# Attention, experts and an MLP on one core: k and v loaded six tokens per partition, with new times in the attention's step list

## The chip, the cores and the metric

The kernel runs on one core of a Trainium2 chip. TensorE (PE, with its weight loads shown as PEld), VectorE (DVE), ScalarE (ACT), GpSimd (POOL) and SyncE (SP) run their own instruction lists in order and wait for one another at semaphores; DMA queues move data between DRAM and the cores' memory of 128 partitions. The metric is the device time of one execution in microseconds (us).

## The reference

Three stages follow one another: a linear attention over 4 batches of 8 heads with 576 tokens of 64 channels, a mixture of 8 experts that gives each of the 2,304 tokens to one expert, and an MLP with a softplus.

```python
kv  = einsum('bhsd,bhse->bhde', k, v)            # 64 x 64 for each head
out = einsum('bhsd,bhde->bhse', q, kv)
x   = out / sqrt(mean(out*out, -1) + 1e-6) * g_norm      # -> [2304, 512]

xn = x / (norm(x) + 1e-6)
logits = xn @ (emb / (norm(emb) + 1e-6)).T / tau          # 8 experts
e = argmax(logits); gate = softmax(logits)[e]
y = gate * (relu(x @ w1[e]) @ w2[e])                      # 512 -> 1024 -> 512

h = y @ w_in                                              # 512 -> 2048
out = (max(h, 0) + log1p(exp(-abs(h)))) @ w_out
```

All arrays are float32. The sum over tokens in kv takes the 576 tokens in any order and grouping.

## The kernel before

**Loads.** All loads of attention go through SP's queue in the order of the code: `load_kv(0, 4)`, q of batch 0 in two halves, k and v of batch 1 in two halves of four heads each, q of batch 1, and so on. A k or v tile is [128, 8 heads, 4*64]: 512 tokens, four on a partition, which is a piece of 1,024 bytes in DRAM. The rest of 64 tokens comes in tiles of its own, kr and vr, [64, 8, 64], in pieces of 256 bytes. Two buffers each serve four batches.

**Steps.** `kv_mm` sums a head's kv in PSUM: four matmuls with 128 rows (L295) and one with 64 (L296). `kv_fin` brings kv of a batch into kvx in six small steps ("fin") on ACT, DVE and PE. A tile t is 128 tokens; there are 18, of which tiles 8 and 13 are "mixed", made of the last 64 tokens of two batches. Each tile goes through q (a copy on DVE, L337), tr (transposes on PE), qs (a copy on ACT), o (matmuls with kvx, L354, or L358 for a mixed tile), sq (squares, ACT), cp (copy to oc, ACT), ss (sums, DVE, L371). Pairs of tiles then get a Newton step for the inverse root (n, DVE), lt and lg (logits, DVE), xa (the normalised tile, on POOL, written to the DRAM tensor xd as well), xo (times g_norm, **on POOL or DVE**, L410) and nn (squares of xo, ACT). `route(g)`, after each six tiles, finds the expert of each token (top-1, slots, tokens, on DVE and PE); behind the last one, ranks and indices make rk_e, the experts sorted by size, and rk_idx, the table of token rows of each expert (L541).

**The order.** Each step is entered with its engine, a time that it is supposed to cost, what it depends on, and for some an earliest time `at`, taken from the table `LATE`. `list_schedule` plays these numbers through and gives each step a begin and, for xo, an engine; the steps are then emitted in order of begin. On the chip nothing of these numbers remains but the order on each engine and the choice for xo. An xo that would end on POOL behind a threshold (53,000 in the table's ns) is put off by 10,000 there, so that DVE gets it.

**Behind attention.** POOL gathers the token rows of the first expert from xd by rk_idx, in three indirect DMAs into xgt (`gather`, L1038). SP loads weight pieces st once rk_e is known. PE transposes the gathered rows (`first_transposes`, L1068), ACT and DVE split them into xh and xl (L1072, L1076), weights are split into wh and wl (L857, L859), and from there PE multiplies experts and then the MLP to the end. Attention's tiles come from the pools hp and tp, which are closed at its end; xgt and st come from later pools that take the same memory over, opened with `reuse_waits="tile"`: the first writer of such a tile waits for the last instructions that used the old tiles lying there. Where a tile lies follows from the sizes allocated before it.

Of the kernel before, what the change touches and what calls it, by code (L numbers as in the profile page):

```python
# [11 lines left out]
F32 = mybir.dt.float32  # L12
# [13 lines left out]
def attention_moe_mlp(tc, q, k, v, g_norm, emb, tau, w1, w2, w_in, w_out, out, caps=CAPS):  # L26
# [7 lines left out]
    nc = tc.nc  # L34
# [145 lines left out]
    with ExitStack() as hs:  # L180
# [1 line left out]
        tp = hs.enter_context(tc.tile_pool(name="tp", bufs=1))  # L182
        ps = hs.enter_context(tc.tile_pool(name="ps", bufs=1, space=PSUM))

        kt, vt, qt, kr, vr, qr = {}, {}, {}, {}, {}, {}

        def load_kv(b, cuts=1):
            for dst, rem, nm in ((kt, kr, "k"), (vt, vr, "v")):
                dst[b] = hp.tile([128, H, 4 * D], F32, name=f"{nm}{b}", tag=f"{nm}{b % 2}")
                rem[b] = hp.tile([64, H, D], F32, name=f"{nm}r{b}", tag=f"{nm}r{b % 2}")  # L190
            for u in range(cuts):
                hs_ = slice(u * H // cuts, (u + 1) * H // cuts)
                for dst, rem, src in ((kt, kr, k), (vt, vr, v)):
                    nc.sync.dma_start(out=dst[b][:, hs_, :], in_=src[b, hs_, 0:512, :].rearrange("h (p c) d -> p h (c d)", c=4))
                    if u == 0:
                        nc.sync.dma_start(out=rem[b], in_=src[b, :, 512:576, :].rearrange("h p d -> p h d"))

        def load_q(b, half=None):
            if b not in qt:
# [85 lines left out]
        def kv_mm(b, heads, whole=True):  # L285

            for h in heads:
                key = (b, 0 if whole else h // 4)
                j = h // 2 if whole else h % 4 // 2
                if key not in kvs:  # L290
                    kvs[key] = misc_t[:, 0:4 * D].rearrange("p (j d) -> p j d", d=D) if whole else o_t[h // 4][:, 0:2, 0:D]
                kvo = kvs[key][64 * (h % 2):64 * (h % 2) + 64, j, :]
                for c in range(4):
                    cs_ = slice(c * D, c * D + D)
                    nc.tensor.matmul(kvo, kt[b][:, h, cs_], vt[b][:, h, cs_], start=c == 0, stop=False)  # L295
                nc.tensor.matmul(kvo, kr[b][:, h, :], vr[b][:, h, :], start=False, stop=True)  # L296

        kvts = tp.tile([128, 4, 128], F32, name="kvts")

# [48 lines left out]
        def st_o(t):  # L348

            lo, c = tiles[t]  # L350
            o, qs = o_t[t % 2], qs_t[t % NQS]
            for j in range(4):
                if c is not None:
                    nc.tensor.matmul(o[:, j, 0:144], qs[:, j, :], kvx[lo][:, j, :], start=True, stop=True)  # L354
                else:
                    for u in range(2):
                        us = slice(64 * u, 64 * u + 64)
                        nc.tensor.matmul(o[us, j, 0:144], qs[:, j, us], kvx[lo + u][:, j, :], start=True, stop=True)  # L358
# [218 lines left out]
        def step(key, engs, ns, fn, *deps, at=0, tail=0):  # L577

            steps_[key] = [engs, ns if isinstance(ns, tuple) else (ns,), fn, [d for d in deps if d in steps_], at, tail]

        LATE = {"kv1a": 2700, "kv1b": 5700, "q10": 7150, "q11": 8600, "kv2a": 13000, "kv2b": 15900, "qr0": 17400, "q20": 18850, "q21": 20300,
                "kv3a": 24600, "kv3b": 27600, "qr2": 29000, "q30": 30550, "q31": 32000}
        for b in range(1, B):
            step(("mm", b, 0), "P", 1670, lambda b=b: kv_mm(b, range(0, 4)), ("fin", b - 1, 5), at=LATE[f"kv{b}a"])
            step(("mm", b, 1), "P", 1670, lambda b=b: kv_mm(b, range(4, 8)), ("mm", b, 0), at=LATE[f"kv{b}b"])
            gen_ = kv_fin(b)
            mm = ("mm", b, 1)
            for i, (eng, ns, deps) in enumerate((
                ("A", 264, [mm]), ("D", 331, [mm]), ("P", 435, [("fin", b, 0), ("fin", b, 1)]),
                ("A", 478, [("fin", b, 2)]), ("P", 830, [("fin", b, 3)]), ("D", 131, [("fin", b, 4)]),  # L590
            )):
                step(("fin", b, i), eng, ns, lambda g_=gen_: next(g_), *deps)
# [31 lines left out]
        for t in range(NT):  # L624
            lo, c = tiles[t]
            p = t // 2
            if t > 1:
                if c is not None:
                    step(("q", t), "D", 335, lambda t=t: st_q(t), ("tr", t - NQC), at=LATE.get(f"q{lo}{c // 2}", 0))
                step(("tr", t), "P", 435, lambda t=t: st_tr(t), ("q", t), ("qs", t - 2), at=LATE[f"qr{lo}"] if c is None else 0)  # L630
                step(("qs", t), "A", 478, lambda t=t: st_qs(t), ("tr", t), ("o", t - NQS))
            step(("o", t), "P", 980 if c is not None else 1950, lambda t=t: st_o(t), ("qs", t), ("fin", lo if c is not None else lo + 1, 5), ("cp", t - 2), ("sq", t - 2), ("o", t - 1))
            step(("sq", t), "A", 478, lambda t=t: st_sq(t), ("o", t), ("ss", t - NSQ))
            step(("cp", t), "A", 531, lambda t=t: st_cp(t), ("o", t), ("lt", p - NOC), ("xa", 2 * (p - NOC)), ("xa", 2 * (p - NOC) + 1))
            step(("ss", t), "D", 610, lambda t=t: st_ss(t), ("sq", t), ("n", p - NSS, 2))
            if t % 2:
                step(("rs", p), "A", 460, lambda p=p: st_rs(p), ("ss", t - 1), ("ss", t), ("n", p - NSS, 2))
                gen_ = st_newton(p)
                for i in range(3):
                    step(("n", p, i), "D", 85, lambda g_=gen_: next(g_), ("rs", p) if i == 0 else ("n", p, i - 1), ("xa", 2 * (p - NSS)), ("xa", 2 * (p - NSS) + 1))  # L640
                step(("lt", p), "D", 202, lambda p=p: st_lt(p), ("n", p, 2), ("cp", t - 1), ("cp", t), ("lg", p - 2))
                step(("lg", p), "D", 202, lambda p=p: st_lg(p), ("lt", p))
                for u in (t - 1, t):
                    step(("xa", u), "G", 1001, lambda u=u: st_xa(u), ("n", p, 2), ("cp", u), ("xa", u - 1), tail=12000 if u == NT - 1 else 0)
                for u in (t - 1, t):
                    step(("xo", u), "GD", (1225, 560), lambda eng, u=u: st_xo(u, eng), ("xa", u), ("nn", u - NXO))
                    step(("nn", u), "A", 613, lambda u=u: st_n(u), ("xo", u))
            if t in ends:
                route(ends[t])

        def list_schedule():

            after = {k: [] for k in steps_}
            for k, v in steps_.items():
                for d in v[3]:
                    after[d].append(k)
            path = {}

            def length(k):
                if k not in path:  # L660
                    path[k] = steps_[k][1][0] + 180 + max(max((length(n) for n in after[k]), default=0), steps_[k][5])
                return path[k]

            free, begin, end, where = dict.fromkeys("PADG", 0), {}, {}, {}
            todo = dict.fromkeys(steps_)
            while todo:
                ready = []
                for k in todo:
                    engs, ns, _, deps, at, _ = steps_[k]
                    if all(d in end for d in deps):  # L670
                        best = None
                        for eng, n in zip(engs, ns):
                            lag = [end[d] + (220 if where[d] != eng else 0 if eng == "P" else 130) for d in deps]
                            t0 = max([free[eng], at] + lag)
                            if k[0] == "xo" and eng == "G" and t0 + n > 53000:

                                t0 += 10000
                            if best is None or t0 + n < best[3]:
                                best = (t0, k, eng, t0 + n)
                        ready.append(best)  # L680
                t0, k0, eng, t1 = min(ready, key=lambda r: (r[0], -length(r[1])))
                t0, k0, eng, t1 = max((r for r in ready if r[2] == eng and r[0] <= t0 + SLACK), key=lambda r: (length(r[1]), -r[0]))
                if k0[0] in ("nn", "xo"):

                    soon_ = [r for r in ready if r[2] == eng and r[0] < t0 + HOLD * (t1 - t0) and r[1][0] not in ("nn", "xo")]
                    if soon_:
                        t0, k0, eng, t1 = min(soon_, key=lambda r: r[0])
                begin[k0], end[k0], where[k0] = t0, t1, eng
                free[eng] = t1
                del todo[k0]  # L690
            return begin, where
# [696 lines left out]
```

## Time and profile before

| | |
|---|---|
| median of 3 runs | 761.85 us (760.89 to 762.2) |
| profiled execution | 759.51 us |
| its span, first to last instruction | 757.7 us |
| PE busy | 721.7 us (95%) |
| DVE, ACT, POOL busy | 531.3, 419.2, 269.4 us |
| DMA | 96.70 MB, 128 GB/s on average |
| attention, up to the index table | the first 92.6 us |

Busy shares over the whole span hide the stages: attention and the passage to the first expert make up the first 105 us, experts and MLP the rest. Times in the rows below are counted from the start of the span. A row `36.45 0.68 PE L295 ... x8` is a group of eight instructions of one line that starts at 36.45 and lasts 0.68 us; on PE the modelled ends overlap the next start, so what one costs is read from start to start. A float32 matmul of the program appears as two in the trace (x8 for four).

### The profile page before, as it was taken

The page shows a single profiled execution, that of the slowest core. Times are in us where ns is not written, and L with a number is a line of the kernel's source. Part 1 is how long each engine was busy: PE and PEld are TensorE (multiplying, and loading weights), DVE is VectorE, ACT ScalarE, POOL GpSimd, SP SyncE. Part 2 cuts the span into 40 slices and gives each one's busy share as a digit, 9 for nine tenths or more (in the row PEclk, how much of TensorE's full clock was granted, in tenths as well). Part 3 has the DMA queues.
Part 4 walks back from the last instruction along what each step waited for, and adds up shares of the span by engine and source line. Part 5 has one row for each costly group of instructions (what it writes and reads, how often), then busy time and mean ns, then how long its engine had stood idle before and what let it go on. Part 6 is the DMA issues. An engine that isn't in the chain of part 4 may idle for free.

```text
span 757.7 us, 11972 instructions
## 1 busy us (share of the span) xinstructions
PE 721.7 (95%) x4370; PEld 658.3 (87%) x4370; DVE 531.3 (70%) x1019; ACT 419.2 (55%) x821; POOL 269.4 (36%) x199
## 2 busy tenths in 40 slices
PE   9999269999999999998999999999999999999996
PEld 5888149989999999998999999999999989898985
DVE  4568977788787887897897565756665666575653
ACT  2657556646566576564765544644554464455443
POOL 3245645776776877673660100100010010001001
PEclk9999589999999999999999999999999999999998
DMA  9994298798988989941220100100010000001001
GB/s 237 266 257 173 85 342 272 248 294 265 297 276 283 303 272 314 292 135 43 98 84 1 42 1 0 43 1 1 0 43 1 1 28 15 1 0 43 1 1 45
DMA packets 71073, 96.70 MB, mean 128 GB/s; under 512 B 13010, under 2 KB 45802, under 8 KB 71008
## 3 DMA queue, kind: packets, MB, share of 16 engines
q1 hardware_dynamic: 67488, 86.02, 36.7%
q0 software_dynamic: 3344, 9.80, 3.6%
q8 instruction: 36, 0.59, 0.3%
q14 instruction: 29, 0.24, 0.1%
q10 hardware_dynamic: 176, 0.05, 0.0%
HBM read 78.01 MB, written 17.84 MB: 126 GB/s over the span
## 4 chain that ended last, share of the span: by engine, by line
PE 45%; issue 8%; DVE 1%; POOL 1%; ACT 0%; DVEq 0%; POOLq 0%
PE tp_t L853 8%; PE tp_t L852 8%; PE tp_t L851 8%; PE acc_t L957 7%; PE acc_t L956 7%; PE acc_t L955 7%; POOL out_dram L962 1%; DVE xsl L867 0%; DVE own L1265 0%; PE acc_t L853 0%; PE acc_t L851 0%; PE acc_t L852 0%; DVE eu L926 0%; ACT eu L923 0%; DVE x L1222 0%
## 5 line engine op out<-in xcount | busy, mean ns | idle before, releaser
L859 POOL TENSOR_TENSOR wl<-st,wh 128x1024 fp32r<-128x1024 f32 x66 | 159.0, 2410 | 74.7 <-ACT wh L857 73.9
L962 POOL DMA_INDIRECT out_dram<-orow,idx x18 | 19.9, 1103 | 337.2 <-ACT orow L961 333.8
L922 ACT ACTIVATE e<-tp_t 128x384 f32<-128x384 f32 x93 | 45.7, 492 | 127.8 <-PE tp_t L853 127.8
L924 DVE TENSOR_SCALAR u<-e 128x384 f32<-128x384 f32 x94 | 33.8, 360 | 112.5 <-ACT e L923 111.7
L857 ACT CAST wh<-st 128x1024 fp32r<-128x1024 f32 x72 | 75.2, 1048 | 44.8 <-POOL wl L859 17.4
L851 PE MATMUL acc_t<-hh,wh 128*128 128x368 f32 (+7 forms) x256 | 81.2, 317 | 1.2 <-DVE hl L1207 1.2
L851 PE MATMUL acc_t<-xh,wh 128*128 128x368 f32 (+7 forms) x256 | 78.6, 307 | 0.3 <-ACT x L1224 0.3
L852 PE MATMUL acc_t<-xl,wh 128*128 128x368 f32 (+7 forms) x256 | 78.2, 306 | 0.0
L853 PE MATMUL acc_t<-xh,wl 128*128 128x368 f32 (+7 forms) x256 | 78.0, 305 | 0.0
L853 PE MATMUL acc_t<-hh,wl 128*128 128x368 f32 (+7 forms) x256 | 78.0, 305 | 0.0
L852 PE MATMUL acc_t<-hl,wh 128*128 128x368 f32 (+7 forms) x256 | 78.0, 305 | 0.0
L930 ACT ACTIVATE u<-u 128x384 f32<-128x384 f32 x94 | 49.5, 526 | 50.0 <-DVE e L926 49.3
L852 PE MATMUL tp_t<-xsl,wh 128*128 128x384 f32 x192 | 64.6, 336 | 0.7 <-DVE xsl L867 0.7
L853 PE MATMUL tp_t<-xsh,wl 128*128 128x384 f32 x192 | 64.8, 337 | 0.0
L851 PE MATMUL tp_t<-xsh,wh 128*128 128x384 f32 x192 | 64.7, 337 | 0.0
L940 DVE TENSOR_TENSOR gl<-u,gh 128x384 fp32r<-128x384 f32 x94 | 60.2, 640 | 6.0 <-ACT gh L938 6.0
L853 PE MATMUL tp_t<-xsh,wl_b 128*128 128x384 f32 x188 | 63.4, 337 | 0.0
L851 PE MATMUL tp_t<-xsh,wh_b 128*128 128x384 f32 x188 | 63.3, 337 | 0.0
L852 PE MATMUL tp_t<-xsl,wh_b 128*128 128x384 f32 x188 | 63.2, 336 | 0.0
L957 PE MATMUL acc_t<-wh,gl 128*128 128x512 f32 x144 | 57.1, 397 | 1.6 <-DVE gl L940 1.6
L931 DVE SCALAR_TENSOR_TENSOR u<-tp_t,u 128x384 f32<-128x384 f32 x93 | 51.7, 556 | 9.9
L933 DVE TENSOR_TENSOR u<-u,e 128x384 f32<-128x384 f32 x94 | 56.0, 595 | 3.2
(254 smaller groups left out, 1880.3 us busy)
## 6 DMA issues: line engine op xcount, KB each, us to landing
st<-in_moe_w_dram SPq DMA_DIRECT2D x64, 512.0 KB
raw<-in_moe_w_in_dram SPq DMA_DIRECT2D x16, 512.0 KB
raw<-in_moe_w_out_dram SPq DMA_DIRECT2D x16, 512.0 KB
wd<-pre_p SPq DMA_DIRECT2D x32, 256.0 KB
q<-in_q_dram SPq DMA_DIRECT2D x8, 512.0 KB
xd<-xa SPq DMA_DIRECT2D x16, 256.0 KB
st<-wd SPq DMA_DIRECT2D x8, 512.0 KB
raw<-wd SPq DMA_DIRECT2D x8, 512.0 KB
```

Of the source, the lines that this page charges most:

```text
L851: nc.tensor.matmul(ps_, wh, xh, start=start, stop=False)
L852: nc.tensor.matmul(ps_, wh, xl, start=False, stop=False)
L853: nc.tensor.matmul(ps_, wl, xh, start=False, stop=stop)
L857: nc.scalar.copy(h, raw)
L859: eng.tensor_tensor(out=l, in0=raw, in1=h.bitcast(F32), op=ALU.subtract)
L930: nc.scalar.activation(out=u, in_=u, func=AF.Ln)
L931: nc.vector.scalar_tensor_tensor(out=u, in0=h, scalar=0.0, in1=u, op0=ALU.max, op1=ALU.add)
L933: nc.vector.tensor_tensor(out=u, in0=u, in1=e, op=ALU.subtract)
L940: nc.vector.tensor_tensor(out=gl, in0=u, in1=gh.bitcast(F32), op=ALU.subtract)
L955: nc.tensor.matmul(mt[b][t_], gh[:, cs_], wh[:, f % 2, :], start=f == 0, stop=False)
L956: nc.tensor.matmul(mt[b][t_], gh[:, cs_], wl[:, f % 2, :], start=False, stop=False)
L957: nc.tensor.matmul(mt[b][t_], gl[:, cs_], wh[:, f % 2, :], start=False, stop=f == NF - 1)
```

## The change

k and v tiles become [96, 8, 6*64]: six tokens on each of 96 partitions, a piece of 1,536 bytes, and all 576 tokens. The tiles of the rest and their eight DMAs go. A head's kv is six matmuls with 96 rows. The k and v tiles (two buffers each) take 12,288 bytes of a partition each instead of 8,192 and 2,048 for the rest. In the step list, the two kv steps of a batch are entered at 3,700 instead of 1,670, o at 1,180 (mixed: 1,500) instead of 980 (1,950), the threshold for xo on POOL is 60,000, and `LATE` has other times for kv, q and qr.

```diff
+        CK = 6
+        SK = S // CK
         def load_kv(b, cuts=1):
-            for dst, rem, nm in ((kt, kr, "k"), (vt, vr, "v")):
-                dst[b] = hp.tile([128, H, 4 * D], F32, name=f"{nm}{b}", tag=f"{nm}{b % 2}")
-                rem[b] = hp.tile([64, H, D], F32, name=f"{nm}r{b}", tag=f"{nm}r{b % 2}")
+            for dst, nm in ((kt, "k"), (vt, "v")):
+                dst[b] = hp.tile([SK, H, CK * D], F32, name=f"{nm}{b}", tag=f"{nm}{b % 2}")
             for u in range(cuts):
                 hs_ = slice(u * H // cuts, (u + 1) * H // cuts)
-                for dst, rem, src in ((kt, kr, k), (vt, vr, v)):
-                    nc.sync.dma_start(out=dst[b][:, hs_, :], in_=src[b, hs_, 0:512, :].rearrange("h (p c) d -> p h (c d)", c=4))
-                    if u == 0:
-                        nc.sync.dma_start(out=rem[b], in_=src[b, :, 512:576, :].rearrange("h p d -> p h d"))
+                for dst, src in ((kt, k), (vt, v)):
+                    nc.sync.dma_start(out=dst[b][:, hs_, :], in_=src[b, hs_].rearrange("h (p c) d -> p h (c d)", c=CK))
...
-                for c in range(4):
+                for c in range(CK):
                     cs_ = slice(c * D, c * D + D)
-                    nc.tensor.matmul(kvo, kt[b][:, h, cs_], vt[b][:, h, cs_], start=c == 0, stop=False)
-                nc.tensor.matmul(kvo, kr[b][:, h, :], vr[b][:, h, :], start=False, stop=True)
+                    nc.tensor.matmul(kvo, kt[b][:, h, cs_], vt[b][:, h, cs_], start=c == 0, stop=c == CK - 1)
...
-        LATE = {"kv1a": 2700, "kv1b": 5700, "q10": 7150, "q11": 8600, "kv2a": 13000, "kv2b": 15900, "qr0": 17400, "q20": 18850, "q21": 20300,
+        LATE = {"kv1a": 1700, "kv1b": 5800, "q10": 8000, "q11": 10200, "kv2a": 14300, "kv2b": 18400, "qr0": 19800, "q20": 22000, "q21": 24200,
...
-            step(("mm", b, 0), "P", 1670, lambda b=b: kv_mm(b, range(0, 4)), ("fin", b - 1, 5), at=LATE[f"kv{b}a"])
+            step(("mm", b, 0), "P", 3700, lambda b=b: kv_mm(b, range(0, 4)), ("fin", b - 1, 5), at=LATE[f"kv{b}a"])
...
-                            if k[0] == "xo" and eng == "G" and t0 + n > 53000:
+                            if k[0] == "xo" and eng == "G" and t0 + n > 60000:
```

How the lists change is seen at three places. The first is PE, before: the end of route 0's slot matmuls (oh_all is the chosen expert of each token), behind which the first kv matmuls of batch 3 stand (k3, v3). The mixed tile 8 stands before both, 21 rows up.

```order
L450 MATMUL rt_234<-oh_all_114,ones_68 128x16
L450 LDWEIGHTS ones_68
L450 MATMUL rt_234<-oh_all_114,ones_68 128x8
L295 MATMUL misc_233<-v3_211,k3_209 64x64 x4
L296 MATMUL misc_233<-vr3_212,kr3_210 64x64
```

The same place on PE, after: both kv steps of batch 3 (24 matmuls each), and then the mixed tile 8 (L357).

```order
L353 MATMUL o0_213<-kvx1_225,qs2_246 128x144 x4
L342 MATMUL qp1_216<-ident_70,qc3_243 128x128 x4
L295 MATMUL misc_217<-v3_198,k3_197 64x64 x24
L353 MATMUL o1_214<-kvx1_225,qs3_247 128x144 x4
L342 MATMUL qp0_215<-ident_70,qr0_191 128x128 x4
L295 MATMUL misc_217<-v3_198,k3_197 64x64 x24
L357 MATMUL o0_213<-kvx0_223,qs0_244 64x144
```

The kv matmuls of batch 3 have moved ahead of tile 8 and of route 0's slots. The second place is DVE at the end of attention, before: the index table and the xo products of the last two tiles, then the first row of what follows.

```order
L533 TENSOR_TENSOR pt_1079<-tab_311,perm_315 128x192
L541 TENSOR_REDUCE rk_idx_107<-pt_1079 128x24
L410 TENSOR_TENSOR xo6_291<-xa16_276,g_rep_227 128x512
L410 TENSOR_TENSOR xo7_292<-xa17_277,g_rep_227 128x512
L700 TENSOR_TENSOR below_1087<-rank_314,io8_79 128x64
```

DVE there, after:

```order
L532 TENSOR_TENSOR pt_1088<-tab_295,perm_299 128x192
L540 TENSOR_REDUCE rk_idx_107<-pt_1088 128x24
L409 TENSOR_TENSOR xo2_271<-xa12_256,g_rep_211 128x512
L409 TENSOR_TENSOR xo3_272<-xa13_257,g_rep_211 128x512
L409 TENSOR_TENSOR xo4_273<-xa14_258,g_rep_211 128x512
L409 TENSOR_TENSOR xo5_274<-xa15_259,g_rep_211 128x512
L409 TENSOR_TENSOR xo6_275<-xa16_260,g_rep_211 128x512
L409 TENSOR_TENSOR xo7_276<-xa17_261,g_rep_211 128x512
L699 TENSOR_TENSOR below_1103<-rank_298,io8_79 128x64
```

Six xo products stand behind rk_idx where two stood. The third place is POOL at the end of attention, before: the last xa, three xo, the three gathers and the first split of weights.

```order
L397 TENSOR_TENSOR xa17_277<-oc2_266,rinv2_306 128x512
L410 TENSOR_TENSOR xo3_288<-xa13_273,g_rep_227 128x512
L410 TENSOR_TENSOR xo4_289<-xa14_274,g_rep_227 128x512
L410 TENSOR_TENSOR xo5_290<-xa15_275,g_rep_227 128x512
L1038 DMA xgt_1128<-xd_60,rk_idx_107 128x512 x2
L1038 DMA xgt_1128<-xd_60,rk_idx_107 112x512
L859 TENSOR_TENSOR wl_0_1181<-st0_1132,wh_0_1179 128x1024
```

POOL there, after:

```order
L409 TENSOR_TENSOR xo1_270<-xa11_255,g_rep_211 128x512
L396 TENSOR_TENSOR xa14_258<-oc1_249,rinv1_289 128x512
L396 TENSOR_TENSOR xa15_259<-oc1_249,rinv1_289 128x512
L396 TENSOR_TENSOR xa16_260<-oc2_250,rinv2_290 128x512
L396 TENSOR_TENSOR xa17_261<-oc2_250,rinv2_290 128x512
L1037 DMA xgt_1144<-xd_60,rk_idx_107 128x512 x2
L1037 DMA xgt_1144<-xd_60,rk_idx_107 112x512
L858 TENSOR_TENSOR wl_0_1197<-st0_1148,wh_0_1195 128x1024
```

The three xo products between the last xa and the gathers are gone from POOL. In all, POOL has 11 of the 18 xo products before and 4 after; DVE has 7 and 14.

## Rows read from the trace of the kernel before

**Rows 1.** Busy time by stage: stretch, its length, engines, PE's granted clock, DMA share, GB/s

```profile
core 0: us, PE busy (x) PEld busy (x) DVE busy (x) ACT busy (x) POOL busy (x), PEclk, DMA share, GB/s
45.00:60.00 15.00, 14.13 (x151) 12.45 (x150) 13.76 (x36) 9.04 (x22) 8.94 (x7) 1.00 1.08 268
60.00:76.00 16.00, 14.05 (x135) 12.90 (x133) 14.38 (x40) 13.14 (x31) 9.59 (x9) 1.00 0.41 143
76.00:92.70 16.70, 3.17 (x37) 1.92 (x38) 15.67 (x44) 8.50 (x24) 10.42 (x9) 0.56 0.23 79
92.70:105.20 12.50, 7.63 (x27) 4.07 (x25) 7.31 (x24) 4.59 (x12) 5.58 (x4) 0.64 0.91 285
105.20:380.00 274.80, 268.89 (x1803) 258.72 (x1803) 222.35 (x363) 170.56 (x293) 190.11 (x95) 1.00 0.75 245
```

**Rows 2.** Waits of PE from 0 to 110 us: total, times, longest

```profile
PE acc_t L1068 <- DMA xgt<-xd,rk_idx: 4.9, 1, 4.9
...
PE o L296 <- DMA vr<-in_v_dram: 0.3, 1, 0.3
```

**Rows 3.** Timeline of PE at the kv matmuls of batch 2

```profile
36.45 0.68 PE L295 MATMUL misc<-v,k 128*64 128x64 f32 x8
37.06 0.33 PE L296 MATMUL misc<-vr,kr 64*64 64x64 f32 x2
37.31 0.68 PE L295 MATMUL misc<-v,k 128*64 128x64 f32 x8
```

**Rows 4.** Timeline of PE from attention's last o to the first expert

```profile
73.06 2.44 PE L354 MATMUL o<-kvx,qs 128*128 128x144 f32 x16
...
100.86 1.09 PE L1068 MATMUL acc_t<-ident,xgt 128*128 128x128 f32 x4 [4.87 <-DMA xgt<-xd,rk_idx]
101.74 1.06 PE L177 MATMUL tp_t<-ones 128*128 128x512 bf16 x2
...
104.30 0.58 PE L1068 MATMUL acc_t<-ident,xgt 112*128 112x112 f32 x2
104.68 0.58 PE L1068 MATMUL tp_t<-ident,xgt 112*128 112x112 f32 x2
...
113.91 0.74 PE L760 MATMUL tp_t<-tgb,sel_all 128*128 128x72 bf16 x18 [2.04 <-DVE tgb L756]
```

**Rows 5.** Timeline of DVE from 60 us to behind rk_idx

```profile
60.95 0.42 DVE L308 COPY kvx<-misc 64x256 f32<-64x256 f32 x1 [1.85 <-ACT kvx L306]
...
61.63 0.42 DVE L337 COPY qc<-q 128x512 f32<-128x512 f32 x1
...
63.07 0.95 DVE L337 COPY qc<-q 128x512 f32<-128x512 f32 x1
...
79.53 0.68 DVE L371 TENSOR_REDUCE ss<-sqb 128x8 f32<-128x520 f32 x1
...
87.93 1.08 DVE L460 TENSOR_SCALAR pm<-ci 128x6 int32<-128x6 int32 x1
88.92 0.16 DVE L461 TENSOR_SCALAR pm<-ci 128x6 int32<-128x6 int32 x1
...
89.07 0.94 DVE L464 TENSOR_TENSOR sel_all<-iota_i,pm 128x768 bf16<-128x768 int32 x1
...
92.26 0.35 DVE L541 TENSOR_REDUCE rk_idx<-pt 128x24 int32<-128x192 f32 x1
92.53 1.28 DVE L410 TENSOR_TENSOR xo<-xa,g_rep 128x512 f32<-128x512 f32 x2
93.73 0.21 DVE L700 TENSOR_TENSOR below<-rank,io 128x64 f32<-128x64 f32 x1
```

**Rows 6.** Timeline of POOL at the end of attention

```profile
85.28 3.70 POOL L410 TENSOR_TENSOR xo<-xa,g_rep 128x512 f32<-128x512 f32 x3
92.91 1.34 POOL L1038 DMA_INDIRECT xgt<-xd,rk_idx  x1 [3.94 <-DVE rk_idx L541]
```

**Rows 7.** SP's issues from 92 us, and GB/s from 92 to 106 us in 40 slices

```profile
92.57 2.22 SPq L1023 DMA_DIRECT2D st<-in_moe_w_dram  x4
...
GB/s 0 0 0 0 23 114 255 377 360 383 386 392 348 328 205 167 202 178 222 383 363 389 345 328 404 378 281 211 208 281 290 246 351 375 380 380 380 375 380 410
```

More of the change, by code (lines that the diff above doesn't have):

```diff
@@ L183, in attention_moe_mlp @@
         ps = hs.enter_context(tc.tile_pool(name="ps", bufs=1, space=PSUM))
-        kt, vt, qt, kr, vr, qr = {}, {}, {}, {}, {}, {}
+        kt, vt, qt, qr = {}, {}, {}, {}
+        CK = 6
+        SK = S // CK
         def load_kv(b, cuts=1):
-            for dst, rem, nm in ((kt, kr, "k"), (vt, vr, "v")):
-                dst[b] = hp.tile([128, H, 4 * D], F32, name=f"{nm}{b}", tag=f"{nm}{b % 2}")
-                rem[b] = hp.tile([64, H, D], F32, name=f"{nm}r{b}", tag=f"{nm}r{b % 2}")
+            for dst, nm in ((kt, "k"), (vt, "v")):
+                dst[b] = hp.tile([SK, H, CK * D], F32, name=f"{nm}{b}", tag=f"{nm}{b % 2}")
             for u in range(cuts):
                 hs_ = slice(u * H // cuts, (u + 1) * H // cuts)
-                for dst, rem, src in ((kt, kr, k), (vt, vr, v)):
-                    nc.sync.dma_start(out=dst[b][:, hs_, :], in_=src[b, hs_, 0:512, :].rearrange("h (p c) d -> p h (c d)", c=4))
-                    if u == 0:
-                        nc.sync.dma_start(out=rem[b], in_=src[b, :, 512:576, :].rearrange("h p d -> p h d"))
+                for dst, src in ((kt, k), (vt, v)):
+                    nc.sync.dma_start(out=dst[b][:, hs_, :], in_=src[b, hs_].rearrange("h (p c) d -> p h (c d)", c=CK))
         def load_q(b, half=None):
@@ L579, in step @@
             steps_[key] = [engs, ns if isinstance(ns, tuple) else (ns,), fn, [d for d in deps if d in steps_], at, tail]
-        LATE = {"kv1a": 2700, "kv1b": 5700, "q10": 7150, "q11": 8600, "kv2a": 13000, "kv2b": 15900, "qr0": 17400, "q20": 18850, "q21": 20300,
-                "kv3a": 24600, "kv3b": 27600, "qr2": 29000, "q30": 30550, "q31": 32000}
+        LATE = {"kv1a": 1700, "kv1b": 5800, "q10": 8000, "q11": 10200, "kv2a": 14300, "kv2b": 18400, "qr0": 19800, "q20": 22000, "q21": 24200,
+                "kv3a": 28300, "kv3b": 32400, "qr2": 33800, "q30": 36000, "q31": 38200}
         for b in range(1, B):
-            step(("mm", b, 0), "P", 1670, lambda b=b: kv_mm(b, range(0, 4)), ("fin", b - 1, 5), at=LATE[f"kv{b}a"])
-            step(("mm", b, 1), "P", 1670, lambda b=b: kv_mm(b, range(4, 8)), ("mm", b, 0), at=LATE[f"kv{b}b"])
+            step(("mm", b, 0), "P", 3700, lambda b=b: kv_mm(b, range(0, 4)), ("fin", b - 1, 5), at=LATE[f"kv{b}a"])
+            step(("mm", b, 1), "P", 3700, lambda b=b: kv_mm(b, range(4, 8)), ("mm", b, 0), at=LATE[f"kv{b}b"])
             gen_ = kv_fin(b)
@@ L631, in attention_moe_mlp @@
                 step(("qs", t), "A", 478, lambda t=t: st_qs(t), ("tr", t), ("o", t - NQS))
-            step(("o", t), "P", 980 if c is not None else 1950, lambda t=t: st_o(t), ("qs", t), ("fin", lo if c is not None else lo + 1, 5), ("cp", t - 2), ("sq", t - 2), ("o", t - 1))
+            step(("o", t), "P", 1180 if c is not None else 1500, lambda t=t: st_o(t), ("qs", t), ("fin", lo if c is not None else lo + 1, 5), ("cp", t - 2), ("sq", t - 2), ("o", t - 1))
             step(("sq", t), "A", 478, lambda t=t: st_sq(t), ("o", t), ("ss", t - NSQ))
```

## The prediction

> **What bounds the kernel now.** I read the windows by stage first [rows 1]. From 45 to 60 us the matrix engine (PE) is busy 14.13 of 15 us and VectorE (DVE) 13.76, so both are full. From 60 to 76 DVE is the fuller (14.38 of 16), and from 76 to 92.7 PE does almost nothing (3.17 of 16.7) while DVE is busy 15.67. From 92.7 to 105.2 neither is busy: this is the gather for the first expert. Behind 105.2 PE is busy again (268.89 of 274.8 us to 380), in code that the change leaves alone. So three things bound in turn: PE to about 60, DVE to the end of the index table rk_idx, then a gather through DRAM, then PE. What the change does to attention counts only as far as it moves rk_idx or the gather.
>
> PE's list of waits [rows 2] says what PE lacks. The largest single one, 4.9 us, is for the gathered rows xgt. For loads of k and v it waits once, 0.3 us at the start; all later ones are ahead of PE.
>
> The rows of DVE [rows 5] and POOL [rows 6] show the hand-over: rk_idx is written from 92.26 to 92.61, POOL issues the gather at 92.91 (0.30 later), and the first transpose of gathered rows runs at 100.86 [rows 4], 7.95 us after the issue.
>
> **The change, part by part.**
>
> *Matmuls of kv.* Before, four 128-row matmuls start 0.61 us ahead of the 64-row one, 0.152 each, and the 64-row one takes 0.25 to the next head's start [rows 3]: 0.86 a head. After, six matmuls of 96 rows. No row has 96; the nearest are the transposes [rows 4], where four of 112 rows and 112 columns take 0.38 per pair (0.19 each) and those of 128 take 0.22 each, so the time goes with the columns and fewer rows cost nothing extra. I take 0.152: 0.91 a head, +0.05 over 32 heads, **+1.4 us on PE**. Below: 0.114 (rows in proportion), −5.7 us. Above: 0.25 as the 64-row ones, +20 us. The +1.4 lies on PE before 60 us, where PE is full, but PE's last o matmuls end at 75.5 [rows 4], and DVE, which is behind with its rows, comes to the last ss that needs them at 79.53 [rows 5]. Less than about 4 us on PE thus stays hidden behind DVE's queue, and I put it at 0; without that cover it costs 1.4.
>
> *Loads.* Eight small DMAs of 64 tokens go, and k and v (9.4 MB of the 14.2 MB that are loaded) come in pieces of 1,536 bytes instead of 1,024 and 256. As PE waits for no load now [rows 2], a faster one gives nothing. A slower one is a rival.
>
> *The order on DVE from 60 us to rk_idx.* The new times and costs push PE's two kv steps of batch 3 ahead of the mixed tile 8 and of route 0's slot matmuls (the order rows of PE). DVE's answers move with them, and this is the part that a table of times hides. Counting DVE rows between that point and rk_idx, after against before: two more ss reductions (0.68 long as at 79.53; they and the xo products follow one another at 0.60): +1.2; route 0's slot chain, which before was done by 57.9, now falls in the stretch: one sel row at 0.94 and eight short ones at about 0.2 (as pm at 88.92): +2.5, an estimate; one more xo product: +0.6 (two take 1.20, from 92.53 to 93.73); one q copy (0.42) and one kvx copy (0.42) that are done before it: −0.8, of which I count −0.7 by their pitch [rows 5]. Sum **+3.6** of work.
>
> Against it stand two things. DVE idles 1.85 us for kvx just before 60.95; of that 0.95 lies after 60, and with DVE's work queued up it is filled: **−1.0**. And DVE is stretched by POOL: a q copy takes 0.95 at 63.07 and 0.42 at 61.63; pm takes 1.08 at 87.93, while POOL's three xo products run (85.28 to 88.98), and 0.16 at 88.92 when POOL is idle [rows 5, 6]. Between the first and the last of these two rows I count 11 such stretched DVE rows, their excess over the shortest row of their kind summing to 8.8 us. POOL works 9.59 + 10.42 = 20.0 us in the stretch [rows 1]; after, four xo products fewer run on it there (the order rows of POOL), some 1.3 us each: 5.2 us or 26% less, so **−2.3** of the 8.8. Bounds: half of the stretch goes (−4.4), or none of it. Sum for rk_idx: 3.6 − 1.0 − 2.3 = **+0.3 us** (−1.8 to +2.6).
>
> *The gather.* Here is the largest term, and the diff doesn't show it. The four k and v tiles grow from 10,240 bytes a partition (with their rests) to 12,288, so all that is allocated behind them moves up by 8 KB. The gather's buffer xgt lies in memory that attention's pool gives back: before on xa0 to xa3, whose last readers were long done; after on xa14 to xa17, whose last readers are their xo products. Those are now on DVE, six in a row right behind rk_idx, where two stood before (the order rows of DVE); four of them left POOL, where three xo products stood at the tail. In the built programs the first gather waits, before, for DVE's rk_idx; after, for the sixth xo. What is queued behind it on POOL is the other two gathers and wl of the first weights; PE waits for them. The price: the six start 0.08 before rk_idx's end as modelled [rows 5], five steps of 0.60 and a last one of 0.68 make 3.68, so the gather starts **+3.6 us** behind where it stood. Lower bound by the rows: none, as the six can't run in less than their pitch; upper: +4.6 if one of them is stretched by 1 us.
>
> *The landing.* The gather's rows then share the DMA queues with the weight loads that SyncE issues from 92.57 on: eight of 512 KB, moved at 330 to 410 GB/s from 93.4 on [rows 7], about 12 us. A gather issued 3.6 us later meets less of them. If it met none, its 0.75 MB would take some 2 us less; it still meets the last ones, so I take **−0.4** (0 to −2).
>
> *Behind the gather* the chains shift with it: transposes, xh and xl, then the gate table, whose PE wait of 2.04 us at 113.91 [rows 4] ends on DVE rows that are queued behind xl. Four more xo products ahead on DVE (+2.4) end before the gathered rows come.
>
> Sum: 0.3 + 3.6 − 0.4 = **+3.5 us**; the profiled execution took 759.51 us (a span of 757.7 and 1.8 around it), so 763.0. That execution lies 2.34 below the median of the runs, 761.85; on the median's scale the sum gives **765.3 us**. Ends: −1.8 + 3.6 − 2.0 = −0.2 and +2.6 + 4.6 = +7.2, or 761.6 to 769.1.
>
> **Rivals.**
>
> *Faster: DVE's tail shrinks by more than the gather waits.* The place is DVE between 60 and rk_idx. From 83.9 on its rows are one serial chain (top-1, slots, ranks, index), and three stretched ones stand in it; after, POOL has no xo products there. To be faster by more than 0.2% of the time (1.5 us, about what a measurement of this kernel can tell from no change; I use this bound throughout), rk_idx must come at 92.6 − 3.2 − 1.5 = 87.9 or earlier: more than half of the 8.8 us must go and the added 3.6 us of work must find idle time. With all stretches gone, the idle gone and 1 us of the work hidden: 3.6 − 1 − 1 − 8.8 = −7.2, net −4.0, about **758**. Against it: POOL still makes ten or so xa products, and these stretch DVE too. Chance 0.15.
>
> *No change: the later gather is absorbed.* PE's wait of 2.04 us at 113.91 is not for gathered rows but for the gate table on DVE. If that table comes no later than now, the wait shrinks by what PE comes later: 3.5 − 2.0 = +1.5, **763.3**; together with a landing that meets few weight loads, no change. For it: the table's inputs are ready at rk_idx and nn. Against: DVE takes its rows in order behind xl, and behind six xo products. Chance 0.18.
>
> *Slower loads.* With 96 of 128 partitions written, each k and v transfer could run at three quarters. From 45 to 60 us loads move 268 GB/s at a full DMA share [rows 1]; 9.4 MB at this rate take 35 us, a third more is +11.7 us by the last q. PE, with its 4 us in hand, would wait for k3, v3 and q3, and rk_idx would be 6 to 8 us late: **772**. For it: the queues are full to 57 us. Against: pieces are longer, and small ones are gone. [...] No row of this trace loads 96 partitions. Chance 0.07.
>
> *96-row matmuls as dear as 64-row ones:* +20 us on PE before 60, about 6 to 15 of it beyond DVE's slack, **775**. Against: the 112-row transposes. Chance 0.03.
>
> **How the numbers follow.** My forecast, slower by about 3.5 us, has 0.57; its own range is 761.6 to 769.1. Of its cases about one in ten stays within 1.5 us. Faster: the first rival and a little of the forecast's lower end, 0.15. Same (760.3 to 763.4): the second and that tenth, 0.22. Slower: the rest, 0.63. The range takes in half of the first rival and leaves out the last two: 759.5 to 769.5.
>
> **What would show it.** In the changed kernel's profile: kv heads on PE at 0.91 us without a second row of 64; no long PE wait for k or v; DVE's rk_idx ending between 90.8 and 95.2; right behind it one row of xo x6 of about 3.7 us; the gather on POOL some 3.9 us behind rk_idx's end, its wait put down to DVE xo; PE's first transpose 7.5 to 8 us behind that issue; the later stages as long as now. I am wrong if the gather follows rk_idx at 0.3 us, if rk_idx comes before 88 or if PE waits for k3.

## The result, and the profile after

The changed kernel takes 772.24 us (median of 4 runs, 771.02 to 774.52) against 761.5 of the kernel before (4 runs, 760.89 to 762.2): a ratio of 1.0145, 95% interval 1.0128 to 1.0163. It is slower by 10.7 us, three times what was forecast and outside the range. In a later set of runs it took 769.88 (6 runs) beside 762.24 of before, a ratio of 1.011 (1.0085 to 1.0135).

The profiled execution took 774.52 us with a span of 772.7. Busy time by stage, as in [rows 1]:

```profile
core 0: us, PE busy (x) PEld busy (x) DVE busy (x) ACT busy (x) POOL busy (x), PEclk, DMA share, GB/s
45.00:60.00 15.00, 11.78 (x121) 11.24 (x120) 8.82 (x21) 6.39 (x15) 3.35 (x3) 0.86 1.17 229
60.00:76.00 16.00, 15.87 (x178) 14.85 (x177) 11.63 (x31) 13.36 (x31) 4.54 (x4) 0.92 0.58 186
76.00:92.70 16.70, 8.07 (x64) 7.09 (x65) 16.15 (x46) 11.96 (x31) 10.46 (x11) 0.71 0.38 126
92.70:105.20 12.50, 6.40 (x33) 2.50 (x32) 11.39 (x43) 4.74 (x14) 2.87 (x3) 0.56 0.42 144
```

The first row tells the most. Loads move 229 GB/s where they moved 268, at a full DMA share in both (1.17 and 1.08), and PE and DVE, which were full there, are not: DVE does 8.82 us of work instead of 13.76. The work comes later: DVE is full only from 76 us on. PE's list of waits from 0 to 120 us (compare [rows 2]):

```profile
PE acc_t L1067 <- DMA xgt<-xd,rk_idx: 8.1, 1, 8.1
PE misc L295 <- DMA v<-in_v_dram: 7.3, 4, 3.2
...
PE o L295 <- DMA v<-in_v_dram: 1.6, 2, 1.2
```

PE waits 8.9 us for v, where it waited 0.3 (for vr). The timeline of PE shows where, and what a kv group costs (48 rows are 24 matmuls, four heads):

```profile
25.43 2.48 PE L295 MATMUL misc<-v,k 96*64 96x64 f32 x48
29.34 2.48 PE L295 MATMUL misc<-v,k 96*64 96x64 f32 x48 [1.43 <-DMA v<-in_v_dram]
31.74 1.09 PE L342 MATMUL qp<-ident,qc 128*128 128x128 f32 x8
...
43.59 2.45 PE L295 MATMUL misc<-v,k 96*64 96x64 f32 x48 [2.02 <-DMA v<-in_v_dram]
...
55.21 3.81 PE L295 MATMUL misc<-v,k 96*64 96x64 f32 x48 [3.22 <-DMA v<-in_v_dram]
58.96 2.29 PE L353 MATMUL o<-kvx,qs 128*128 128x144 f32 x8
...
83.55 2.27 PE L353 MATMUL o<-kvx,qs 128*128 128x144 f32 x8
```

From 29.34 to 31.74 four heads take 2.40 us, 0.60 each: not 0.91 as forecast but less than the 0.86 of [rows 3]. PE has less to do and is late all the same: its last o starts at 83.55 instead of ending at 75.5 [rows 4]. Behind the wait of 3.22 us the same group takes 3.75 us (55.21 to 58.96). The windows of these two groups give the granted clock, 0.58 there (0.50 from 56.0 to 59.0) and 1.00 at the earlier group:

```profile
55.20:59.00 3.80, 3.79 (x49) 3.68 (x49) 3.59 (x9) 0.00 (x0) 2.79 (x3) 0.58 1.23 170
29.30:31.70 2.40, 2.37 (x48) 2.34 (x48) 1.88 (x4) 0.27 (x1) 1.54 (x2) 1.00 1.21 263
```

DVE's timeline shows its own wait and the end of attention, POOL's the gather (the second fence):

```profile
63.33 0.69 DVE L370 TENSOR_REDUCE ss<-sqb 128x8 f32<-128x520 f32 x1 [3.99 <-ACT sqb L360]
...
99.57 0.35 DVE L540 TENSOR_REDUCE rk_idx<-pt 128x24 int32<-128x192 f32 x1
99.84 3.69 DVE L409 TENSOR_TENSOR xo<-xa,g_rep 128x512 f32<-128x512 f32 x6
103.45 0.22 DVE L699 TENSOR_TENSOR below<-rank,io 128x64 f32<-128x64 f32 x1
```

```profile
103.83 1.17 POOL L1037 DMA_INDIRECT xgt<-xd,rk_idx  x1 [9.42 <-DVE pn L702]
```

The profile puts the gather's wait down to the DVE row that ran when it ended (pn); the sixth xo ends at 103.53, 0.30 before the gather starts.

PE's first transpose of gathered rows runs at 111.98, 11.1 us behind [rows 4]. That is rk_idx 7.3 us late (99.92 against 92.61), the gather 3.91 instead of 0.30 behind it (+3.6), and 8.15 instead of 7.95 us from there (+0.2). From that transpose to the end this execution takes 660.7 us and that of before 656.8, in the same code. The changed kernel run again takes 658.5 there and the other kernels of this study 657.6 to 659.0, so most of the 3.9 is scatter of these two executions; that none of it belongs to the change is not shown.

### The profile page after: what moved, and what is told of

Same layout as the page of the kernel before. It is cut to its first block, busy times and chain, and to the rows that moved or that the text cites. A ratio compares the mean times of both kernels' runs of the same rounds, so it can differ in the third digit from the quotient of the medians.

```text
span 772.7 us, 12086 instructions
## 1 busy us (share of the span) xinstructions
PE 724.5 (94%) x4434; PEld 665.3 (86%) x4434; DVE 534.4 (69%) x1026; ACT 419.9 (54%) x821; POOL 258.7 (33%) x192
## 4 chain that ended last, share of the span: by engine, by line
PE 44%; issue 8%; DVE 1%; POOL 0%; ACT 0%; DVEq 0%; POOLq 0%
PE tp_t L852 7%; PE tp_t L851 7%; PE tp_t L850 7%; PE acc_t L956 7%; PE acc_t L955 7%; PE acc_t L954 7%; POOL out_dram L961 0%; DVE xsl L866 0%; DVE own L1264 0%; PE acc_t L852 0%; PE acc_t L850 0%; PE acc_t L851 0%; DVE eu L925 0%; ACT eu L922 0%; DVE x L1221 0%
```

## The experiments

The table has every complete kernel that ran, one profiled execution of each: PE's waits for v (and its rest) up to 120 us, PE's granted clock from 7 to 60 us, the end of rk_idx, the time from there to the gate-table matmuls that stand at 113.91 in [rows 4], and the median. "w" marks kernels in which the gather waits for xo products. The medians of before in the four sets of runs were 761.25, 761.06, 762.28 and 762.24. A load's landing, where it is given below, is the time at which the trace has its semaphore complete.

| kernel | wait v | clock | rk_idx | to gate | median |
|---|---|---|---|---|---|
| before | 0.3 | 1.00 | 92.61 | 21.30 | 761.5 |
| changed, w | 8.9 | 0.83 | 99.92 | 25.11 | 772.24 |
| changed, again, w | 9.9 | 0.87 | 97.12 | 23.96 | 769.88 |
| new loads, old order, w (two xo) | 3.5 | 0.88 | 96.30 | 23.88 | 766.24 |
| new loads, old order, no w | 5.7 | 0.87 | 96.76 | 21.39 | 766.33 |
| old loads, new order | 0.7 | 1.00 | 91.40 | 22.21 | 759.59 |
| changed, xgt elsewhere | 9.3 | 0.77 | 100.52 | 21.60 | 767.25 |
| the same, again | 7.3 | 0.77 | 103.16 | 21.74 | 768.60 |
| changed, fills beside, w | 5.0 | 1.00 | 96.96 | 24.41 | 769.17 |
| changed, q by heads, w | 2.4 | 0.87 | 98.37 | 24.17 | 770.38 |
| rest padded | 4.8 | 0.97 | 88.18 | 22.07 | 756.12 |
| padded, q by heads | 0 | 0.97 | 86.91 | 21.74 | 755.07 |
| padded, new order | 7.3 | 1.00 | 90.66 | 21.59 | 760.32 |

**Loads or order?** Two kernels each have one half of the change: the changed tiles with the old table, costs and threshold, and the old tiles with the new ones.

> The changed tiles and matmuls with the table, the costs and the threshold of before. Theory A (loads onto 96 partitions run at about three quarters of their rate, PE waits for v): PE waits for v about 7 to 9 us again, rk_idx is 5 to 8 us late, the gather waits for two xo products instead of six; 768 to 771 us. Theory B (the new order costs the time, the loads little): 761 to 764 us.

> The tiles, loads and matmuls of before with the new table, costs and threshold. Theory A: no waits for v; six xo products behind rk_idx, but xgt lies on xa0 to xa3, so the gather follows rk_idx at 0.3 us; 760 to 764 us. Theory B: 768 to 772 us.

766.24 us, 1.0056 (1.0033 to 1.0079), and 759.59, 0.9979 (0.9958 to 1.0001). So the loads cost, and the order by itself does not. The landing of the last half of v shows the loads directly: 52.15 us in the kernel with the old loads (53.67 in the kernel before), 59.16 in the one with the new, and between 58.8 and 62.1 in all kernels of the table that have the new ones. Both miss their numbers: the second by 0.4 us, the first by 2 us, since with the old order PE comes to its kv groups later and waits 3.5 us instead of 8.9.

**The gather's wait.** xgt is put back on early tiles by the order in which xa is laid out:

```diff
-        xa_t = {i: tp.tile(...) for i in [*range(7, NT), *range(7)]}
+        xa_t = {i: tp.tile(...) for i in [*range(7, 14), *range(4), *range(14, NT), *range(4, 7)]}
```

> The changed kernel, with the xa tiles laid in another order so that the gather's buffer lies on xa0 to xa3. If the wait for six xo products costs what it lasts: the gather follows rk_idx at 0.3 us and the time falls by 3.6 us, to 768.6. If the later gather was hidden behind weight loads or the gate table: 771 to 772.

The gather then follows at 0.30 us (100.52 to 100.82):

```profile
100.82 1.34 POOL L1037 DMA_INDIRECT xgt<-xd,rk_idx  x1 [5.81 <-DVE rk_idx L540]
```

The median is 767.25, 5.0 less than the changed kernel's first one, which stands in another set of runs. A pair with the old order disagreed, so this kernel was run again beside the changed one:

> The changed tiles and matmuls with the table, costs and threshold of before, and xa laid so that the gather's buffer lies on xa0 to xa3: of the change only loads and matmuls are left. The gather then follows rk_idx at 0.3 us instead of 2.1, so about 2 us less than the 766.2 of the kernel with the wait: 763.5 to 765.5, some 3 us above before, all of it in rk_idx. If the later gather was hidden: 766.

> The changed kernel itself, as the measure for the other two on the same chip: 770.5 to 773.5 us.

> The changed kernel with the gather's buffer on xa0 to xa3 once more, beside the changed kernel itself. If the wait of the gather for six xo products costs what it lasts: 3 to 5 us less than the changed kernel in the same call. If it is taken up behind the gather, as two medians of the old order suggest: less than 1.5 us.

768.60 beside 769.88 for the new order, and 766.33 against 766.24 for the old (1.0052 and 1.0056 of before, in different sets of runs; there the gather waits 1.85 us longer): by the medians the wait costs 1.3, 5.0 or nothing. The changed kernel itself came out below the 770.5 to 773.5 that were expected. The traces say why the medians are a poor measure here: rk_idx alone moves by 6 us between executions of kernels whose instructions are the same up to there (97.12 to 103.16). In part v comes at another time (its last half lands at 60.20 and at 62.11 in these two), in part PE runs at another clock (0.87 and 0.77; see the last experiment). The stage behind rk_idx is free of this. From rk_idx to the gate table it takes 21.3 to 22.2 us in all eight kernels without the wait, and 24.0 to 25.1 in the four with six xo products, a mean of 24.4 against 21.7. The wait costs **2.7 us** of its 3.6; the rest is given back by the landing: in three of the four the third group of transposes stands 10.6 to 10.9 us behind the gather's issue (11.6 in the fourth), against 11.7 and 11.8 in the same kernel without the wait.

Without the wait, the new loads and matmuls cost 1.0052 of before with the old order and 1.0073 and 1.0078 with the new one. The new order on top of the new loads thus costs some 1.6 to 2.0 us; the intervals overlap, so this part is not clear of noise.

**What slows the loads?** It can be the length of the pieces, the number of partitions or which partitions they are. Two kernels load k and v with nothing beside it. The timeline of DVE shows, for each stretch of loads, the copy that waits for all of them; the idle time in brackets is the stretch. Each kernel ran once; a form that stands twice in it repeats within 1 us.

> Loads of k and v alone, all computation left out (the output is zeros): eight stretches, each of 16 loads of half a batch through SyncE's queue, each stretch waiting for the one before: twice 128 partitions in pieces of 1,024 bytes (8.4 MB), 128 partitions in pieces of 1,536 bytes (9.4 MB), partitions 0 to 95 (1,536), partitions 32 to 127, heads in turn on 0 to 95 and 32 to 127, and then again 128 and 0 to 95. [...]

```profile
54.44 0.22 DVE L38 COPY seen<-buf 32x64 f32<-32x64 f32 x1 [26.52 <-DMA buf<-in_v_dram]
82.88 0.22 DVE L38 COPY seen<-buf 32x64 f32<-32x64 f32 x1 [28.22 <-DMA buf<-in_v_dram]
123.42 0.22 DVE L38 COPY seen<-buf 32x64 f32<-32x64 f32 x1 [40.32 <-DMA buf<-in_v_dram]
163.12 0.22 DVE L38 COPY seen<-buf 32x64 f32<-32x64 f32 x1 [39.49 <-DMA buf<-in_v_dram]
200.63 0.22 DVE L38 COPY seen<-buf 32x64 f32<-32x64 f32 x1 [37.28 <-DMA buf<-in_v_dram]
```

128 partitions: 8.4 MB in pieces of 1,024 bytes in 26.5 us, 9.4 MB in pieces of 1,536 in 28.2. Partitions 0 to 95: 40.3 us, and 32 to 127: 39.5. So the pieces are not it; larger ones were the faster (334 against 316 GB/s by these times). Heads in turn on 0 to 95 and 32 to 127 gained little (37.3 us): two transfers behind one another on one queue don't make up for each other's partitions here, and why is open. That left how many partitions or which, and the second kernel tells these apart:

> Loads alone, all computation left out (the output is zeros): seven stretches of 16 loads of about 0.59 MB (8.3 MB in all for 112 partitions, 9.4 MB else), all in pieces of 1,536 bytes, onto partitions 0 to 127, 0 to 95, 0 to 63, 32 to 95, 64 to 127, 0 to 111, and 0 to 127 again. [...]

```profile
28.71 0.20 DVE L44 COPY seen<-buf 32x48 f32<-32x48 f32 x1 [27.80 <-DMA buf<-in_v_dram]
68.94 0.20 DVE L44 COPY seen<-buf 32x48 f32<-32x48 f32 x1 [40.03 <-DMA buf<-in_v_dram]
116.84 0.20 DVE L44 COPY seen<-buf 32x48 f32<-32x48 f32 x1 [47.70 <-DMA buf<-in_v_dram]
145.58 0.20 DVE L44 COPY seen<-buf 32x48 f32<-32x48 f32 x1 [28.54 <-DMA buf<-in_v_dram]
194.65 0.20 DVE L44 COPY seen<-buf 32x48 f32<-32x48 f32 x1 [48.87 <-DMA buf<-in_v_dram]
227.97 0.20 DVE L44 COPY seen<-buf 32x48 f32<-32x48 f32 x1 [33.12 <-DMA buf<-in_v_dram]
```

In order: 0 to 127, 0 to 95, 0 to 63, 32 to 95, 64 to 127, 0 to 111. The same 9.4 MB go onto 64 partitions in 47.7 us if these are 0 to 63, in 48.9 if they are 64 to 127, and in 28.5, nearly as fast as onto all 128, if they are 32 to 95. It is which partitions, not how many. Of the rate of 128, 32 to 95 ran at 0.97, 0 to 111 (8.3 MB, 250 GB/s) at 0.73, 0 to 95 at 0.69, 0 to 63 at 0.58 and 64 to 127 at 0.57. What lies behind this order no run shows.

**The price of a kv matmul.** The kernel before with the rest of 64 tokens in tiles of 128 partitions, the upper half zeroed once, so that all matmuls have 128 rows (and xa in the order shown above):

```diff
-                rem[b] = hp.tile([64, H, D], F32, name=f"{nm}r{b}", tag=f"{nm}r{b % 2}")
+                rem[b] = hp.tile([128, H, D], F32, name=f"{nm}r{b}")
+                nc.gpsimd.memset(rem[b][64:128], 0.0)
...
-                        nc.sync.dma_start(out=rem[b], in_=src[b, :, 512:576, :]...)
+                        nc.sync.dma_start(out=rem[b][0:64], in_=src[b, :, 512:576, :]...)
```

> The kernel before with its loads, but the rest of 64 tokens lies in tiles of 128 partitions whose upper half is zeroed once, so that a head's kv is five matmuls of 128 rows; a rest tile for each batch; xa in the order that keeps the gather's buffer on xa0 to xa3. If the 64-row matmul is dear because the number of rows changes and changes back: 0.50 us a head instead of 0.86, 11 us less on PE before 60 us, and with the loads as before 752 to 760 us. If a matmul simply costs by its rows (0.152 for 128, 0.100 for 96): 0.76 a head, 3 us less on PE, hidden; 760 to 763 us.

756.12 us, 0.9929 (0.9907 to 0.9951): faster than both kernels. The timeline of PE at the second kv group of batch 1, four heads (40 rows; those between the first and the last are left out):

```profile
25.82 0.73 PE L296 MATMUL misc<-v,k 128*64 128x64 f32 x10
...
27.55 0.28 PE L297 MATMUL misc<-vr,kr 128*64 128x64 f32 x2
27.76 1.09 PE L344 MATMUL qp<-ident,qc 128*128 128x128 f32 x8
```

1.94 us for 20 matmuls, 0.097 each. A matmul of 96 rows costs 0.100 and one of 128 the same; the 0.86 of a head before are five of these and 0.36 us that a matmul of 64 rows among those of 128 adds. Part of it stands ahead of the 64-row one: the four before it take 0.61 [rows 3], here 0.39. No run has 64-row matmuls in a row, so a price of the change of height and a 64-row matmul that is dear by itself are not told apart.

**Are the loads the pace?** q by heads is loaded in pieces of 1,024 bytes instead of 512:

```diff
-            lo, hi = (0, 4) if half is None else (2 * half, 2 * half + 2)
...
+            hs_ = slice(4 * half, 4 * half + 4)
+            nc.sync.dma_start(out=qt[b][:, hs_].rearrange("p h c d -> p h (c d)"), in_=q[b, hs_, 0:512, :].rearrange("h (p c) d -> p h (c d)", c=4))
```

> The changed kernel, with q of a batch loaded in two halves of four heads (pieces of 1,024 bytes) instead of two halves of two tokens (512 bytes). In the traces q moves at 200 to 215 GB/s and pieces of 1,024 bytes at about 340, so 4.2 MB of q take some 8 us less of the queues. If the load stream sets rk_idx of the changed kernel: PE's waits for v shrink by more than half, rk_idx comes 4 to 8 us earlier and the time is 764 to 768 us. If the loads are only a symptom and the order sets the end: 771 to 773.

> The kernel with padded rests, and q loaded by heads. If its waits for v (4.2 us) come from the load stream: they go, rk_idx comes 2 to 5 us earlier, 751 to 754 us. If DVE's own work from 45 us on bounds it: 755 to 757.

> The kernel with padded rests, with the changed kernel's table, costs and threshold. The order alone gave 0 to 1.6 us with the loads of before; here PE is ahead and waits for v already, so I expect no more than that: 754 to 757 us; if kv placed early makes PE wait longer for v, 757 to 760.

On the changed kernel the waits for v shrink to 2.4 us, but 770.38 is a miss: PE now waits 3.6 us at 35.77 for kvx and 2.6 at 18.61 for a q copy on DVE, which itself waited 3.3 us for q, since a tile's q is complete only with the second half. The wait moved. On the padded kernel no wait for v is listed any more and rk_idx comes 1.3 us earlier; 755.07 (0.9916 of before, 0.9892 to 0.994) can't be told from 756.12. The new order on the padded kernel costs some 4 us (760.32, 0.9989 of before, 0.9969 to 1.001; rk_idx 2.5 us later): it asks for kv early, and PE waits 7.3 us for v instead of 4.8.

The padded kernels also give the price of the loads with fast matmuls on both sides and the gather without its wait. With the new order the loads of before take 760.32 (0.9989) and the new ones 767.25 and 768.60 (1.0073 and 1.0078); with the old order 756.12 (0.9929) and 766.33 (1.0052). That is 0.8 to 1.2%, 6 to 9 us, of which the 96-row matmuls, 0.115 us a head dearer, could explain at most 3.7.

**Does the low clock cost by itself?** Dummy matmuls ahead of kv groups keep PE busy in its waits.

> The changed kernel, with dummy matmuls of ones (128 x 512) ahead of six groups of kv matmuls on PE, into the PSUM tile that these then overwrite, so that PE is busy where it waited for v. If the low granted clock behind the waits costs by itself: PE's clock stays near 1.00 from 19 to 60 us, kv of the last batch and rk_idx come 2 to 5 us earlier, 767 to 770 us. If only the arrival of v counts: no earlier, 771 to 774.

That kernel's fills overwrote half of kv, so it computes something else, and its time (5,057 us) tells nothing. Its trace up to rk_idx can still be read: clock 0.97, rk_idx 98.49. Beside kv's half of the tile:

```diff
+            for _ in range(FILL.get((b, u), 0)):
+                nc.tensor.matmul(misc_t[:, 256:512], ones, ones.unsqueeze(1).to_broadcast([128, 2, 128]), start=True, stop=True)
             kv_mm(b, range(4 * u, 4 * u + 4))
...
-        fill(w_, 2)
+        fill(w_, 8)
```

> The changed kernel, with dummy matmuls of ones (128 x 256) ahead of five groups of kv matmuls, into the half of the PSUM tile that kv doesn't use, and six more fills at the start, so that PE is busy where it waited for v. If the low granted clock behind the waits costs by itself: PE's clock stays near 1.00 from 19 to 60 us, kv of the last batch and rk_idx come 2 to 5 us earlier, 767 to 770 us. If only the arrival of v counts: no earlier, 771 to 774.

The clock from 7 to 60 us, in windows of the changed kernel run again, and of this one:

```profile
7.00:60.00 53.00, 42.19 (x480) 38.73 (x480) 26.40 (x69) 21.01 (x49) 8.89 (x10) 0.87 1.16 232
```

```profile
7.00:60.00 53.00, 46.32 (x571) 41.14 (x569) 26.21 (x69) 20.98 (x49) 8.88 (x10) 1.00 1.15 238
```

The clock is full, DVE does the same 26 us of work, and rk_idx comes at 96.96 against 97.12; 769.17 us against 769.88. The time lies in the range for a clock that costs, but so does the changed kernel beside it. In this pair a PE at full speed waits for the same v, and the clock costs nothing that can be told.

That does not hold for every execution. In the second one with xgt elsewhere (0.77 from 7 to 60 us) the kv groups of batches 1 and 2 take 4.2 us each instead of 2.4, those of batch 2 at a granted clock of 0.50. The second fence is the changed kernel run again, where only those of batch 1 are so slow.

```profile
42.09 4.25 PE L295 MATMUL misc<-v,k 96*64 96x64 f32 x48 [3.05 <-DVE r L147]
...
47.31 4.28 PE L295 MATMUL misc<-v,k 96*64 96x64 f32 x48
...
59.22 2.48 PE L295 MATMUL misc<-v,k 96*64 96x64 f32 x48
```

```profile
54.82 2.45 PE L295 MATMUL misc<-v,k 96*64 96x64 f32 x48 [2.78 <-DMA v<-in_v_dram]
```

The last row of each is the first kv group of batch 3, 4.4 us apart. Its v has landed at 57.19 in the first and at 54.69 in the second: 2.5 of the 4.4 us are v, and 1.9 are PE, which was still behind with its slow groups. (The 3.05 us at 42.09 are a wait for v as well, which landed at 41.95; with them the 7.3 of the table are 10.4.) So the lower clock behind the waits costs something where PE comes later than v; no run fills the waits of such an execution, so how much is open.

## Why the prediction was wrong

**The step that failed is the loads.** The sum has no term for them, since PE "waits for no load now" and "a faster one gives nothing. A slower one is a rival", and that rival got 0.07. It was the case. Loads onto partitions 0 to 95 ran at 0.69 of the rate, the last half of v landed at 60.62 instead of 53.67, PE waited 8.9 us for v, and rk_idx came 7.3 and 4.5 us late in the two executions. That is the rival's mechanism (three quarters of the rate, PE waiting, rk_idx 6 to 8 us late). Its three quarters was the author's estimate from 96 of 128 partitions, and no run shows it: in the loads alone 0 to 95 ran at 0.69 and 0.70 of the rate of 128, 32 to 127 at 0.71 and 32 to 95 at 0.97. That the first median also meets its 772 is in part luck: the same kernel took 769.88 later. The case against it, longer pieces and no small ones, was true of pieces and didn't weigh: the queues were full [rows 1], so that any loss of rate had to show, and "No row of this trace loads 96 partitions" should have widened the range instead of closing the question.

**The term of the matmuls** had the wrong sign: +1.4 us forecast (its own 0.05 over 32 heads is 1.6), 0.86 to 0.60 a head or −8.3 us measured. The error was to divide 0.61 by 4 as the price of a 128-row matmul: four of them take 0.39 where no 64-row one follows, so the 0.61 held part of what that one adds. Unlike matmuls can't be priced by dividing. On the new loads the gain only brought PE to its waits sooner; on the loads of before a larger one does shorten the kernel (756.12), though PE waits 4.8 us for v there too.

**The order on DVE** was put at +0.3 with the loads as before. The kernel with old loads and new order has rk_idx at 91.40, −1.2: within the stated bounds, and the new order alone is not slower. But the term was read for a PE that waits for no load. Where PE does wait, the new order costs: some 4 us on the padded kernel, perhaps 2 on the new loads.

**The gather** was right in place and size: it starts 3.6 us later behind six xo products of 3.69 us. The landing was given −0.4; the stage behind gives back 0.9. Its reading of [rows 7] was too smooth: the loads do not run at 330 to 410 GB/s throughout but drop to 167 to 222 for five slices in a row.

**Sum by the runs.** rk_idx +4.5 to +7.3 (two executions of the changed kernel) and 2.7 from the gather's wait make 7.2 to 10.0 us; measured, 7.6 and 10.7. That the ends meet so well is partly chance, since rk_idx is known from one execution of each set and moves by some us. What sets the time at which v arrives, and the clock, from one execution to the next stays open.

## What to carry to other kernels

Before k or v is laid onto fewer than 128 partitions, ask which partitions: the same bytes took 28.5 us on 32 to 95 and 47.7 on 0 to 63, and in a stream of loads that was already full (a DMA share of 1.08) the last half of v landed at 60.62 instead of 53.67. Matmuls of one height in a row, of 96 or of 128 rows, took 0.10 us each here; one of 64 rows among those of 128 added 0.36 to a head, and the kernel that pads it with zeros took 756.12 us against the 761.25 of before. And when tiles grow, look at what now lies under the buffers of the next stage: a wait can appear where no line was changed.

## What was not expected of the hardware

64 partitions loaded nearly as fast as 128 where they were 32 to 95 (28.5 against 27.8 us for 9.4 MB), and took 47.7 us where they were 0 to 63. Pieces of 1,536 bytes ran faster than those of 1,024 (9.4 MB in 28.2 us against 8.4 in 26.5). Float32 matmuls of 96 and of 128 rows with 64 columns cost the same 0.10 us, and a 64-row one among those of 128 added 0.36 to a head of five.
